# Splitting each output weight tile of part 2 into a low and a high half

## The chip, the cores and the metric

The kernel runs on one core of one Trainium2 chip. The metric is device time in microseconds (us) of one launch, as the median of several runs; the profile is one more execution, taken by the hardware profiler. A core has five engines that work beside each other, each with its own instruction queue: TensorE (PE in the profile, with its weight loads as PEld), VectorE (DVE), ScalarE (ACT), GpSimd (POOL) and SyncE (SP), which here issues nearly all DMAs. The tensors lie in the chip's memory (DRAM); the engines work on SBUF, and matmuls write to PSUM.

## The reference

`reference()` chains three stages, all float32:

```
k_p, v_p = mean of k, v over 8 neighbours along seq         # batch 8, heads 8, seq 576, dim 64
attn     = softmax(q @ k_p.T / 8) @ v_p
x        = attn as 4608 tokens x 512
h        = max(x @ w1, x @ w2, x @ w3); y = h @ w_out       # 512 -> 768 -> 512
out      = relu(y @ w_in) ** 2 @ w_out2                     # 512 -> 2048 -> 512
```

Weights are handed in as 64-bit numbers, which the kernel converts itself.

## The kernel before, in words

Every matmul operand is split in two: a high half rounded to the format the matrix engine reads (`F32R`), and a low half that holds the rest. A product of two split operands is three matmuls: high x high, high x low, low x high. `PARTS` (line 41) holds these pairs (a, c), with a for the stationary operand and c for the moving one; 0 is high and 1 is low.

Part 1 (to about 755 us) does attention and the first feed-forward block. On the side, `prepare_in` and `prepare_out` read the weights of the second block, form the seven combinations that a Strassen-like scheme (7 products in place of 8, for 2 x 2 blocks) needs, split them and store them to DRAM (`wi2_dram`, `wo2_dram`). A `wo2_dram` entry is one combination m for one quarter of the hidden width: 128 partitions x [u][half][256], 4 KB per partition.

Part 2 loops over 9 token blocks j of 512 tokens, and in each over 4 groups gr of the hidden width. `moe2_in` makes the seven input products of a group (84 matmuls of 128 x 256, line 669) and the squared relu of their sums. `moe2_out` then makes the group's output products, in the order of `OUT`: four in groups 0 and 1, ten in groups 2 and 3, so 28 in a block. Each output product

- splits its operand into g (ScalarE writes the high half, line 133, VectorE the low half, line 134; a ring of four);
- takes its weight tile (512 KB, high and low half of both u) from a ring of five, `wo_p`;
- does 12 matmuls (line 799) into one of five accumulators accA to accF: four with g high and weights high, four with g high and weights low, four with g low and weights high.

`fetch_group` puts the loads of the next group's tiles on SyncE's queue (`fetch_out`, line 601). A load waits there until the product that used its buffer is done, since the ring has only five buffers. SyncE also reads the next block's y (`load_y`, line 616, small pieces that follow group 2) and stores the output (line 755). SyncE works in order: whatever stands behind a waiting DMA waits too.

The order of the instructions on each engine isn't the order of the Python code. A planner (`schedule_with_timeline_sim=True`) takes the code's order as priority, simulates the program with its own cost estimates, and gives each engine the next instruction that is ready in that simulation. So input-product matmuls of the next group stand between output products where the planner expected an operand late. On the chip the order is fixed, and an engine waits where an operand is later than planned.

Of the kernel before, what the change touches and what calls it, by code (L numbers as in the profile page):

```python
# [11 lines left out]
F32R = mybir.dt.float32r  # L12
# [8 lines left out]
P = 128  # L21
# [19 lines left out]
PARTS = ((0, 0), (0, 1), (1, 0))  # L41
# [41 lines left out]
def as_f32(ap):  # L83
    return ap.bitcast(F32)
# [8 lines left out]
def attention_moe_kernel(ctx: ExitStack, tc: tile.TileContext, q, k, v, vn, w1, w2, w3, wo1, wi2, wo2, out):  # L93
    nc = tc.nc
# [12 lines left out]
    for sign, base in ((1, POOL * MID), (-1, POOL - 1 - POOL * MID)):  # L107
        nc.gpsimd.affine_select(
            out=sums, in_=sums, compare_op=ALU.is_ge, fill=0.0, base=base,
# [4 lines left out]
    wo2_dram = {  # L114
        (m, g, h): dram.tile([P, 2, 2, 256], F32, name=f"wo2_dram{m}_{g}_{h}")
        for m in range(1, 8) for g in range(2) for h in range(2)
    }
# [14 lines left out]
    def split_to(hi, lo, src, engine):  # L132
        nc.scalar.activation(hi, src, AF.Copy)  # L133
        engine.tensor_tensor(out=lo, in0=src, in1=as_f32(hi), op=ALU.subtract)  # L134

    def split(hl, src, engine=nc.vector):

        split_to(hl[:, 0], hl[:, 1], src, engine)
# [9 lines left out]
    def convert(raw_pool, raw, after=None):  # L148

        low, high = raw[:, :, 0], raw[:, :, 1]
        a = raw_pool.tile([P, 512], I32, tag="row", name="wbits", bufs=3)
        if after is not None:
            nc.gpsimd.tensor_copy(as_f32(a[:1, :1]), after[:1, :1])
        nc.scalar.activation(as_f32(a), as_f32(high), AF.Abs, scale=REBIAS)  # L160
        nc.scalar.activation(low, low.bitcast(U32), AF.Copy, scale=LOW_SCALE, bias=LOW_BIAS)
        nc.vector.scalar_tensor_tensor(
            out=a, in0=a, scalar=3, in1=low, op0=ALU.logical_shift_left, op1=ALU.bitwise_or
        )
        nc.vector.scalar_tensor_tensor(
            out=a, in0=high, scalar=-0x80000000, in1=a, op0=ALU.bitwise_and, op1=ALU.bitwise_or
        )
        return as_f32(a)

    def in_place(raw):  # L170
        return raw.rearrange("p a b -> p (a b)").rearrange("p (c a) -> p c a", c=2).bitcast(F32R)
# [254 lines left out]
    def store_second(dst, w):  # L426
        nc.sync.dma_start(out=dst, in_=as_f32(w))

    def prepare_out(raw, rows, f):

        half = KF2 // 2
        g, u, h = f % half // 4, f // 2 % 2, f % 2

        def store(m, hi, lo):
            for i, w in enumerate((hi, lo)):
                store_second(wo2_dram[m, g, h][:, u, i], w)

        rows.append(convert(raw_p, raw[0], now[0]))
        own = in_place(raw[0])
        l, r = slice(0, 256), slice(256, 512)  # L440
        if f >= half:
            split(own, rows[0], nc.gpsimd)
            store(2, own[:, 0, l], own[:, 1, l])
            store(3, own[:, 0, r], own[:, 1, r])
            return
        b2, b1 = rows
        c = raw_p.tile([P, 512], F32, tag="row", name="wsum", bufs=3)

        def combine(out, in0, in1):
            nc.vector.tensor_tensor(out=out, in0=in0, in1=in1, op=ALU.subtract)  # L450

        combine(c[:, l], b1[:, r], b1[:, l])
        combine(c[:, r], b2[:, r], b1[:, r])
        combine(b1[:, r], b2[:, r], c[:, l])
        combine(b2[:, r], b2[:, l], b1[:, r])
        split(own, b1, nc.gpsimd)
        store(1, own[:, 0, l], own[:, 1, l])
        store(6, own[:, 0, r], own[:, 1, r])
        hi, lo = b1.bitcast(F32R), c.bitcast(F32R)
        split_to(hi, lo, c, nc.gpsimd)  # L460
        store(5, hi[:, l], lo[:, l])
        store(7, hi[:, r], lo[:, r])
        hi, lo = b2[:, l].bitcast(F32R), b2[:, r].bitcast(F32R)
        split_to(hi, lo, b2[:, r], nc.gpsimd)
        store(4, hi, lo)
# [124 lines left out]
    wi2_t, wo2_t, yr_t, y_t = {}, {}, {}, {}  # L590
# [6 lines left out]
            wi2_t[p].append(w)  # L597

    def fetch_out(gr, m, h):
        w = wo_p.tile([P, 2, 2, 256], F32R, tag="wo2", name="wo2s")  # L600
        nc.sync.dma_start(out=as_f32(w), in_=wo2_dram[m, gr % 2, h])
        wo2_t.setdefault((gr, m, h), []).append(w)

    def shared_place(i, shape, name):
        return y_p.tile(shape, F32, tag=f"r{i}", name=name)
# [51 lines left out]
    wo_p = ctx.enter_context(tc.tile_pool(name="wo_p", bufs=5, reuse_waits="tile"))  # L657
# [33 lines left out]
    def moe2_in(j, gr):  # L691

        def unit(h, half):
            if half and gr < NG // 2:
                return shared_place(4 * gr + h, [P, T2], "a21")
            return c_p.tile([P, T2], F32, tag=f"c{2 * half + h}", name=f"c{2 * half + h}")

        def bank():
            return mm_ps.tile([P, T2], F32, tag="ps", name="ps")

        c = {(h, half): unit(h, half) for h in range(2) for half in range(2)}

        def only(m):
            ps = bank()
            product(ps, j, gr, m, first=True)
            return ps

        squared_there = squared_by_scalar if gr == NG - 1 else squared
        nc.scalar.activation(c[0, 0], only(1), AF.Copy)
        add(c[0, 1], only(6), c[0, 0])  # L710
        add(c[1, 0], only(7), c[0, 1])
        y = only(5)
        add(c[1, 1], y, c[1, 0])
        squared_there(c[1, 1])
        add(c[0, 0], only(2), c[0, 0])
        squared_by_scalar(c[0, 0])
        add(c[1, 0], only(4), c[1, 0])
        squared_by_scalar(c[1, 0])
        product(y, j, gr, 3)
        add(c[0, 1], y, c[0, 1])  # L720
        squared_there(c[0, 1])
        return c
# [11 lines left out]
    def operand(gr, m, h, c):  # L734

        k = gr % (NG // 2)
        if m == 7:
            kept[k, h, "s3"] = shared_place(4 * k + 2 + h, [P, T2], "s3")
            kept[k, h, "a21"] = c[h, 1]
            minus(kept[k, h, "s3"], c[h, 0], c[h, 1])  # L740
            return kept[k, h, "s3"]
        if m == 5:
            add(kept[k, h, "a21"], c[h, 1], kept[k, h, "a21"])
            return kept[k, h, "a21"]
        if m == 6:
            minus(kept[k, h, "s3"], c[h, 1], kept[k, h, "s3"])
            return kept[k, h, "s3"]
        if m == 3:
            minus(c[h, 0], c[h, 0], kept[k, h, "s3"])
            return c[h, 0]  # L750
        return c[h, 1 if m == 4 else 0]
# [5 lines left out]
    def evacuate(j, b, n):  # L757

        acc = made[b][0]
        if b in "AB" and n == HALF:  # L760
            q = made["q" + b] = c_p.tile([P, T2], F32, tag="q" + b, name="q" + b)
            nc.scalar.activation(q, acc, AF.Copy)
        if n < FULL[b]:
            return
        q = made["qA"]
        if b == "A":
            o = c_p.tile([P, T2], F32, tag="c3", name="o")
            nc.scalar.activation(o, acc, AF.Copy)
            store_out(j, 0, 0, o)
        elif b == "D":  # L770
            add(q, acc, q)
        elif b == "B":
            o = c_p.tile([P, T2], F32, tag="c2", name="o")
            add(o, acc, q)
            store_out(j, 1, 0, o)
        elif b == "E":
            add(q, acc, q)
            add(made["qB"], made["qB"], q)
            store_out(j, 1, 1, made["qB"])
        else:  # L780
            add(q, acc, q)
            store_out(j, 0, 1, q)
        del made[b]

    def moe2_out(j, gr, m, h, c):

        g = g_p.tile([P, 2, T2], F32R, tag="g", name="g")
        split(g, operand(gr, m, h, c))
        b = BANKS[m]
        if b not in made:  # L790
            made[b] = [acc_ps.tile([P, T2], F32, tag=f"acc{b}", name=f"acc{b}"), 0]
        bank, n = made[b]
        made[b][1] = n + 1
        w = wo2_t[gr, m, h].pop(0)
        k = 0
        for a, c in PARTS:
            for u in range(2):
                for i in range(2):
                    nc.tensor.matmul(  # L799
                        bank[:, i * 256 : (i + 1) * 256], lhsT=g[:, a, u * HT + i * P : u * HT + (i + 1) * P],  # L800
                        rhs=w[:, u, c], start=(n == 0 and k == 0),
                        stop=(n + 1 in (HALF, FULL[b]) and k == 11),
                        skip_group_check=(n >= HALF),
                    )
                    k += 1
        evacuate(j, b, n + 1)

    def fetch_group(gr):
        for m, h in OUT[gr >= NG // 2]:
            fetch_out(gr, m, h)  # L810
# [5 lines left out]
    for j in range(NB2):  # L816
        for gr in range(NG):
            more = j + 1 < NB2
            c = moe2_in(j, gr)
# [55 lines left out]
```

## Time and profile before

| | us |
|---|---|
| median of 3 runs | 1467.53 (1467.47 to 1467.97) |
| the profiled execution | 1472.47 |
| span of its profile | 1470.7 |
| PE busy | 1433.6 (97%) |
| DVE busy | 982.5 (67%) |
| ACT busy | 765.2 (52%) |
| output weight loads | 252 of 512 KB, 5.1 from issue to landing (median) |

The span runs from the first to the last instruction; the execution's own time adds what lies around it. Matmuls are pipelined, so the duration of a single one (some 0.28 us) is more than its share of the time; the pace is read from long runs of them.

### The profile page before, as it was taken

Reading aid. Unit: us, or ns where it says so; the run is one execution under the profiler, and the core shown is the slowest. Engines: PE = TensorE matmul, PEld = TensorE weight load, DVE = VectorE, ACT = ScalarE, POOL = GpSimd, SP = SyncE. Lnnn points to the kernel's source line nnn. Section 1 sums busy time; section 2 is a strip of 40 time slices with the busy share of each in tenths; the row PEclk is TensorE's granted clock in tenths of the full one; section 3 lists DMA queues with packets and bytes.
Section 4 is the critical chain, followed back from the end, with each engine's and each line's share of the span. In section 5 each row is a group of like instructions: output and inputs, shape, how many; then the busy total and the mean of one; then the engine's idle time right before and its main releaser. Section 6 shows DMA issues by size and latency. Waiting matters only on the chain.

```text
span 1470.7 us, 27579 instructions
## 1 busy us (share of the span) xinstructions
PE 1433.6 (97%) x10410; PEld 1411.6 (96%) x10410; DVE 982.5 (67%) x1778; ACT 765.2 (52%) x1983; POOL 180.6 (12%) x228
## 2 busy tenths in 40 slices
PE   7989999999999999999999999999999999999998
PEld 4879999999999999999999999999999999999998
DVE  5896466675675846756336767677777767686775
ACT  7795366665666656664323445354535344454443
POOL 3451022312322312221000000000000000000000
PEclk9999999999999999999999999999999999999999
DMA  6653135433444433333459847565666666565746
GB/s 224 194 164 103 53 132 163 161 105 127 153 151 154 131 134 123 114 101 116 149 189 340 288 152 261 169 232 208 222 226 230 230 215 218 202 228 193 264 150 209
DMA packets 118307, 263.94 MB, mean 179 GB/s; under 512 B 12672, under 2 KB 62848, under 8 KB 118176
## 3 DMA queue, kind: packets, MB, share of 16 engines
q1 hardware_dynamic: 111264, 252.75, 51.3%
q10 hardware_dynamic: 6912, 9.44, 1.8%
q8 instruction: 82, 1.34, 0.4%
q14 instruction: 49, 0.40, 0.1%
HBM read 213.91 MB, written 48.23 MB: 178 GB/s over the span
## 4 chain that ended last, share of the span: by engine, by line
PE 88%; DMA 6%; ACT 3%; DVE 2%; issue 1%; POOL 0%; SPq 0%; DVEq 0%; ACTq 0%; POOLq 0%
PE ps L513 28%; PE ps L669 23%; PE ps L532 10%; PE accB L799 7%; PE accA L799 6%; PE accF L799 3%; DMA wo2s<-wo_dram 3%; PE accE L799 3%; PE accD L799 2%; PE sc L353 2%; PE tr L381 2%; PE av L410 1%; ACT ss L358 1%; PE av L409 1%; DMA wraw<-in_w_dram 1%
## 5 line engine op out<-in xcount | busy, mean ns | idle before, releaser
L513 PE MATMUL ps<-x,w 128*128 128x384 f32 x2592 | 493.9, 341 | 3.0 <-ACT w L133 1.3
L513 PEld LDWEIGHTS ps<-x,w 128*128 128x128 f32 x2592 | 450.6, 189 | 5.6 <-ACT w L133 2.8
L669 PE MATMUL ps<-y,wi2s 128*128 128x256 f32 x3024 | 369.1, 277 | 0.4 <-DVE a L679 0.2
L669 PEld LDWEIGHTS ps<-y,wi2s 128*128 128x128 f32 x3024 | 355.7, 188 | 1.3 <-DVE a L679 0.7
L532 PE MATMUL ps<-h,wo 128*128 128x384 f32 x864 | 161.4, 338 | 2.7 <-POOL wo L134 1.8
L532 PEld LDWEIGHTS ps<-h,wo 128*128 128x128 f32 x864 | 148.9, 188 | 3.4 <-POOL wo L134 2.1
L679 DVE TENSOR_TENSOR c<-ps,c 128x512 f32<-128x512 f32 x144 | 98.5, 689 | 68.1 <-PE ps L669 67.2
L688 ACT ACTIVATE c<-c 128x512 f32<-128x512 f32 x90 | 55.7, 628 | 166.3 <-DVE c L679 165.1
L521 DVE TENSOR_TENSOR hm<-ps,hm 128x384 f32<-128x384 f32 x144 | 79.5, 552 | 69.2 <-PE ps L513 66.9
L133 ACT ACTIVATE g<-c 128x512 fp32r<-128x512 f32 x144 | 90.3, 627 | 63.1 <-DVE c L685 23.3
L799 PE MATMUL accB<-wo2s,g 128*128 128x256 f32 x864 | 113.1, 279 | 8.2 <-DMA wo2s<-wo_dram 6.9
L799 PE MATMUL accA<-wo2s,g 128*128 128x256 f32 x864 | 116.3, 277 | 0.0
L799 PEld LDWEIGHTS accB<-wo2s,g 128*128 128x128 f32 x864 | 105.3, 189 | 9.5 <-ACT g L133 5.4
L134 DVE TENSOR_TENSOR g<-c,g 128x512 fp32r<-128x512 f32 x144 | 98.7, 688 | 18.6 <-ACT g L133 18.5
L799 PEld LDWEIGHTS accA<-wo2s,g 128*128 128x128 f32 x864 | 107.2, 188 | 0.0
L358 ACT ACTIVATE ss<-sc,st 128x72 f32<-128x72 f32 (+1 forms) x320 | 98.1, 320 | 16.8 <-DVE st L355 14.2
L364 POOL TENSOR_TENSOR ss<-ss,st 128x432 f32<-128x432 f32 (+1 forms) x64 | 56.3, 880 | 262.4 <-DVE st L363 174.6
L413 DVE TENSOR_TENSOR xf<-av,xf 64x192 f32<-64x192 f32 (+1 forms) x112 | 50.8, 453 | 46.5 <-ACT xf L412 44.4
L385 DVE TENSOR_TENSOR pt<-tr,pt 72x192 fp32r<-72x192 f32 (+1 forms) x112 | 49.3, 449 | 41.4 <-ACT pt L384 40.2
L412 ACT ACTIVATE xf<-av 64x192 f32<-64x192 f32 (+1 forms) x112 | 45.4, 406 | 54.3 <-PE av L410 39.2
L133 ACT ACTIVATE h<-hm 128x384 fp32r<-128x384 f32 x72 | 37.7, 524 | 66.4 <-DVE hm L521 65.9
L133 ACT ACTIVATE g<-s 128x512 fp32r<-128x512 f32 x72 | 44.7, 630 | 40.9 <-DVE s L682 25.0
(105 smaller groups left out, 1980.3 us busy)
## 6 DMA issues: line engine op xcount, KB each, us to landing
wo2s<-wo_dram SPq DMA_DIRECT2D x252, 512.0 KB, 5.1
wi2s<-wi_dram SPq DMA_DIRECT2D x24, 512.0 KB, 9.0
wraw<-in_wo_dram SPq DMA_DIRECT2D x22, 512.0 KB, 3.8
wraw<-in_w_dram SPq DMA_DIRECT2D x18, 512.0 KB, 3.5
y_dram<-ys ACTq DMA_DIRECT2D x48, 192.0 KB, 2.1
wraw<-in_wi_dram SPq DMA_DIRECT2D x16, 512.0 KB, 3.5
wi_dram<-wraw SPq DMA_DIRECT2D x16, 512.0 KB, 3.8
wo_dram<-wraw SPq DMA_DIRECT2D x64, 128.0 KB, 2.0
```

The lines of the kernel that those rows point to most:

```text
L133: nc.scalar.activation(hi, src, AF.Copy)
L134: engine.tensor_tensor(out=lo, in0=src, in1=as_f32(hi), op=ALU.subtract)
L358: nc.scalar.activation(ss[:, i, h], src[:, i, h], AF.Exp, bias=st[:, 0, i, h : h + 1], accum_out=st[:, 1, i, h : h + 1],)
L364: nc.gpsimd.tensor_tensor(out=ss, in0=ss, in1=st[:, 2].rearrange("p g (h o) -> p g h o", o=1).to_broadcast([m, g, 2, SP]), op=ALU.mult,)
L413: nc.vector.tensor_tensor(out=xf[r], in0=av[r], in1=xf[r], op=ALU.add)
L513: nc.tensor.matmul(ps, lhsT=w1_t[f, e][:, a, kk * P : (kk + 1) * P], rhs=x[kk][:, c], start=(n == 0), stop=(n == 3 * KD - 1),)
L521: nc.vector.tensor_tensor(out=hm, in0=ps, in1=hm, op=ALU.max)
L532: nc.tensor.matmul(ps, lhsT=wo1_t[kk][:, a, d * P : (d + 1) * P], rhs=hs[kk][:, c], start=(n == 0), stop=(n == 3 * KF1 - 1),)
L669: nc.tensor.matmul(bank[:, u * HT : (u + 1) * HT], lhsT=wi2_t[2 * gr + u][i][:, a, o + kk * P : o + (kk + 1) * P], rhs=y_t[j][m][:, c, kk] ...
L679: nc.vector.tensor_tensor(out=out, in0=in0, in1=in1, op=ALU.add)
L688: nc.scalar.activation(c, c, AF.Relu)
L799: nc.tensor.matmul(bank[:, i * 256 : (i + 1) * 256], lhsT=g[:, a, u * HT + i * P : u * HT + (i + 1) * P], rhs=w[:, u, c], start=(n == 0 an ...
```

## The change

Each weight tile becomes two tiles of 256 KB, the low and the high half of its split. They come from two rings (two tags) of five buffers each, which together take as much SBUF as the one ring before. The layout in DRAM changes with it, from [u][half] to [half][u], so that a half is 2 KB in a row per partition. `fetch_out` loads the low half first. The product takes its terms in another order: g high x weights low, g high x weights high, g low x weights high.

```diff
         def store(m, hi, lo):
             for i, w in enumerate((hi, lo)):
-                store_second(wo2_dram[m, g, h][:, u, i], w)
+                store_second(wo2_dram[m, g, h][:, i, u], w)
...
     def fetch_out(gr, m, h):
-        w = wo_p.tile([P, 2, 2, 256], F32R, tag="wo2", name="wo2s")
-        nc.sync.dma_start(out=as_f32(w), in_=wo2_dram[m, gr % 2, h])
-        wo2_t.setdefault((gr, m, h), []).append(w)
+        pair = [None, None]
+        for i in (1, 0):
+            pair[i] = wo_p.tile([P, 2, 256], F32R, tag=f"wo2{i}", name="wo2s")
+            nc.sync.dma_start(out=as_f32(pair[i]), in_=wo2_dram[m, gr % 2, h][:, i])
+        wo2_t.setdefault((gr, m, h), []).append(pair)
...
-        for a, c in PARTS:
+        for a, c in ((0, 1), (0, 0), (1, 0)):
             for u in range(2):
                 for i in range(2):
                     nc.tensor.matmul(
                         bank[:, i * 256 : (i + 1) * 256], lhsT=g[:, a, u * HT + i * P : u * HT + (i + 1) * P],
-                        rhs=w[:, u, c], start=(n == 0 and k == 0),
+                        rhs=w[c][:, u], start=(n == 0 and k == 0),
```

## Rows read from the trace of the kernel before

**Rows 1.** The page's head and its line of the matrix engine.
```profile
span 1470.7 us, 27579 instructions
...
PE 1433.6 (97%) x10410; PEld 1411.6 (96%) x10410; DVE 982.5 (67%) x1778; ACT 765.2 (52%) x1983; POOL 180.6 (12%) x228
```

**Rows 2.** Chain of waits, part 2: start us, us, engine, tile, line, count.
```profile
842.60 8.98 PE ps L669 x79
...
923.62 9.66 PE ps L669 x85
...
936.73 2.72 PE accB L799 x24
...
1000.65 9.66 PE ps L669 x85
```

**Rows 3.** Waits of the matrix engine, 755 to 1471 us: total, times, longest.
```profile
PE accB L799 <- DMA wo2s<-wo_dram: 6.9, 4, 2.8
PE accD L799 <- DMA wo2s<-wo_dram: 1.7, 1, 1.7
PE accF L799 <- DMA wo2s<-wo_dram: 0.9, 3, 0.5
```

**Rows 4.** Timeline of PE, last group of the second block: start, us, instructions, [idle before].
```profile
903.88 1.07 PE L799 MATMUL accB<-wo2s,g 128*128 128x256 f32 x8
...
907.06 0.62 PE L799 MATMUL accA<-wo2s,g 128*128 128x256 f32 x4
...
914.53 1.30 PE L799 MATMUL accB<-wo2s,g 128*128 128x256 f32 x8 [2.78 <-DMA wo2s<-wo_dram]
```

**Rows 5.** Timeline of SP there; chain of waits, two loads from issue to landing.
```profile
906.34 0.32 SPq L601 DMA_DIRECT2D wo2s<-wo_dram  x1
...
907.70 0.80 SPq L601 DMA_DIRECT2D wo2s<-wo_dram  x2
...
907.70 6.69 DMA wo2s<-wo_dram
...
1452.70 4.56 DMA wo2s<-wo_dram
```

**Rows 6.** Line 601, the loads: duration of an issue (ns), issue to landing (us).
```profile
L601 SPq DMA_DIRECT2D wo2s<-wo_dram x252: 319/320/1337, 758.6 to 1459.7; - x126
...
DMA to landing us min/median/max: 3.3/5.1/8.0
```

**Rows 7.** Stretches: us, busy of PE, PEld, DVE, ACT, POOL, PEclk, DMA share, GB/s.
```profile
814.00:818.00 4.00, 3.89 (x34) 3.72 (x33) 2.10 (x4) 0.69 (x2) 0.00 (x0) 1.00 1.03 396
915.00:919.00 4.00, 4.00 (x24) 4.00 (x23) 2.28 (x4) 1.50 (x3) 0.00 (x0) 0.57 0.77 267
1458.00:1462.00 4.00, 4.00 (x23) 4.00 (x23) 0.69 (x1) 0.63 (x1) 0.00 (x0) 0.57 0.72 261
...
907.00:914.00 7.00, 4.75 (x42) 4.55 (x41) 6.88 (x12) 4.04 (x8) 0.00 (x0) 1.00 0.92 265
```

**Rows 8.** Lines 799 and 669: separate wait instructions, count and ns.
```profile
L799 PEldq EVENT_SEMAPHORE  x237: 51/51/51, 767.0 to 1463.0; - x119
...
L669 PEldq EVENT_SEMAPHORE  x48: 51/51/51, 752.5 to 1441.4; - x48
```

**Rows 9.** Third group of block 923.62: SP's issues, SP's wait, PE's tenth product.
```profile
966.14 0.32 SPq L601 DMA_DIRECT2D wo2s<-wo_dram  x1
...
SPq L616 <- DMA wo2s<-wo_dram: 1.4, 1, 1.4
...
975.44 1.09 PE L669 MATMUL ps<-y,wi2s 128*128 128x256 f32 x8
976.37 1.53 PE L799 MATMUL accF<-wo2s,g 128*128 128x256 f32 x12
```

**Rows 10.** DMA of 770 to 784 us and of 962 to 973 us.
```profile
DMA packets 1781, 5.65 MB, mean 404 GB/s; under 512 B 200, under 2 KB 200, under 8 KB 1778
...
DMA packets 1756, 2.94 MB, mean 267 GB/s; under 512 B 189, under 2 KB 1195, under 8 KB 1756
```

## The prediction

> **What bounds the kernel now.** I read four views in this order. The page first: the matrix engine is busy for 1433.6 of 1470.7 us [rows 1], so nothing on another engine or in a queue pays unless it ends an idle stretch of that engine, or brings its clock back. Then the chain of waits, for the length of a token block of part 2. A block begins where a run of 85 input-product matmuls starts: 842.60 and 923.62 are two blocks apart by 81.02 us, 923.62 and 1000.65 by 77.03 us [rows 2]. The 77.03 us block has no wait of the matrix engine in it; 672 matmuls at the pace of its long run (9.66 us / 85 = 113.6 ns) are 76.4 us. So a clean block is at the engine's pace, and a block that is longer has lost the rest. The whole loss of part 2 to output weights is in the third view, the waits of the matrix engine: 6.9 us in accB (4 times), 1.7 in accD (once), 0.9 in accF (3 times), together 9.5 us in 8 waits [rows 3].
>
> The fourth view is the timeline around the longest of them. In the last group of a block (ten products) the seventh product, accB, sat 2.78 us until its weight tile landed [rows 4]. The ring has five tiles, so that tile takes the buffer of the group's second product: accA, whose last 4 matmuls start at 907.06 and are over near 907.7. SyncE issued the load at 907.70, and it landed 6.69 us later; in the last block the same load took 4.56 us [rows 5]. The loop is: a buffer is held for the whole product, the load of 512 KB takes a median 5.1 us (3.3 to 8.0) [rows 6], and five products further on take 5 x 1.36 = 6.8 us (2.72 us for two [rows 2]). Loop and cover are nearly equal, and the jitter of the landing decides. That is why only some blocks wait.
>
> A wait has a second price. The granted clock was 1.00 right after the 1.72 us wait of accD, but 0.57 on average in 915 to 919 us, after the 2.78 us wait, and 0.57 in 1458 to 1462 us, after the last block's wait of 2.00 us [rows 7]; 0.57 is a mix of the 1.2 and the 2.4 GHz level. Each of the two stretches loses 4 x 0.43 = 1.7 us, 3.4 us in all. Block 842.60 to 923.62 agrees: 81.02 - 77.03 = 4.0, against 2.78 + 1.7 = 4.5. So what the output weights cost is 9.5 + 3.4 = 12.9 us, 0.9% of the time. No more can be won from them.
>
> **The change, part by part.**
>
> *Layout in memory and stores.* The stores of part 1 write the same 1 KB per partition to another place in the same 4 KB row. Count, size and order stay; I take 0.
>
> *Order of the terms.* The first eight matmuls of a product still use g's high half and the last four its low half, so the waits for ScalarE and VectorE stay where they are. New is that the low half of the weights is read by the first four matmuls only. Its buffer comes free after a third of the product: in the first product of the group (8 matmuls from 903.88 with others between, and its buffer refilled at 906.34 [rows 4, 5]) near 903.88 + 4 x 0.11 + 0.1 = 904.4 in place of 906.3, 1.9 us sooner; in a product whose 12 matmuls follow each other, 0.9 us sooner. The high half's buffer is free when the whole tile was. And the high half is needed four matmuls, 0.45 us, after the product starts.
>
> *What that does to the waits.* Take the 2.78 us one. The high half of tile 7 goes out at 907.70 as before, but of the 1 MB that was on its way in tiles 6 and 7, the low half of tile 6 (256 KB) has left the queue, and the low half of tile 7 was issued up to 0.9 us before and has partly left. 256 to 512 KB at the 265 GB/s of 907 to 914 us [rows 7] are 1.0 to 2.0 us; I take 1.5. With 0.45 us of later need the wait shrinks by about 1.95 us: 2.78 to 0.8, and the other waits of the last group (0.88, 1.23 and 2.00 us in accB, two of 0.17 us in accF) to nothing. The two in the first block stand in a stretch where the queues run full, 396 GB/s [rows 7]; there an earlier issue is worth less, and I give 0.45 us and half of 0.9 us: 1.72 to 0.8, 0.51 to 0. Left over: 1.6 us of 9.5, so 7.9 us are gained. A wait of 0.8 us is below the 1.72 us that left the clock at 1.00, so both clock losses go: 3.4 us more. Bounds of this part: 0, if the landings move with the issues, to 12.9 us.
>
> *252 more DMA issues.* One costs SyncE 0.32 us [rows 6], 252 x 0.32 = 81 us over some 710 us of part 2. SyncE isn't behind: it issued at 907.70 what came free near 907.7 [rows 4, 5], so its waits for buffers hide this; if they didn't, in a burst of two tiles the last half would go out 2 x 0.45 us later (the pair at 907.70 took 0.80 us for two [rows 5]), which the DMA engines can't use sooner anyway, since 512 KB at 404 GB/s [rows 10] are 1.3 us. I take 0.
>
> *252 more waits on the matrix engine*, one before the fifth matmul of each product. Behind it stand the other eight matmuls, and all that the engine has in order after them. Satisfied, such a wait is carried by the matmul or by a separate instruction of 51 ns: bounds 0 to 252 x 0.051 = 12.9 us. The nearest rows say 0: the output products have 237 of these instructions for 252 products, the input products 48 for 252 [rows 8], and both run at the same pace (2.72 us / 24 = 113.3 ns against 113.6 [rows 2]). I take 0.
>
> *Sum.* The profiled execution took 1472.47 us for its span of 1470.7: 1472.47 - 7.9 - 3.4 = 1461.2 us. The runs' median, 1467.53, is 4.94 us under it. If the profiled execution had 4.94 us of the waits that the timed runs don't have, the runs come to 1461.2 too; if they have all of them, to 1467.53 - 11.3 = 1456.2. The spread of the runs, 0.5 us, shows that what they have repeats, not how much; I lean to the first end: **1460 us**. What is late next is nothing in a clean block; elsewhere it is ScalarE, whose waits at line 799 are under 1 us.
>
> **The rivals.**
>
> *A. The waits move.* The order on each engine is written by a planner from its own estimates of when loads land. In the group before the last, 8 input matmuls stand ahead of the tenth product [rows 9], and 5 ahead of the ninth, although g was ready; I read that as the planner expecting the weights late. With loads that it sees earlier it may take those 13 x 0.11 = 1.5 us out, and the wait of the last group turns up in this one: some 1 us in each of 8 blocks, 8 of the 11.3 us given back. 1464.6 to 1470.4, about 1467. For it: only five tiles fit either way, and bytes per block don't change. Against it: the landing itself gets 1 to 2 us of slack.
>
> *B. Slower: eight DMAs in flight.* In the third group the 128 and 64 KB reads of y stand among the weights. The read issued at 971.64 us had waited 1.4 us for a weight load [rows 9], and the load issued eight DMAs before it is the one of 966.14. So there seems to be a limit of eight, and a half counts as a whole. Between 962.9 and 969.7 us 15 DMAs went out; with halves 20 want to, against 8 in flight at the 3.3 us of the quickest loads [rows 6], 2.4 per us: 8.3 us, so the last half goes out near 971.2 in place of 969.2 and lands 3.3 to 5.1 us later, by 976.3. The tenth product starts at 976.37 [rows 9] and needs it 0.45 us later, so this decides when that landing takes over 5.6 us, or when A takes the cover away as well. Then 1.7 us in each of 8 blocks, 13.6 us, less the gain of 6.3 in the runs: +7, 1475 us. For it: the limit shows, 8.0 us landings exist. Against: the early low halves start before the y reads, and five prefetched tiles cover half of the group.
>
> *C. Smaller transfers are slower.* The first stretch with 512 KB loads moved 404 GB/s, the one with y reads 267 GB/s [rows 10]. If halves went at the second rate, the five late tiles of a group of ten, 2.6 MB, would take 9.8 us in place of 6.5: 3.3 us more in some nine groups, less the gain: up to +20 us, about 1485. Against: these rows differ in what SyncE waits for as well as in size. The Trainium skill (DMA: Bandwidth & Descriptors, Rules for kernel authors) speaks against the change here: it asks for 1 MiB or more per DMA for full bandwidth. By that rule the time would be C's; the trace doesn't bear it out, since loads of half that size already ran at 404 GB/s [rows 10].
>
> *D. It doesn't do what it says:* the planner queues each low half behind the high half before it, which waits for the whole product. The first low half of a group still goes early, so half of the gain stays: 1464.
>
> **Chances.** Forecast 0.52 (own range 1455 to 1463.5), A 0.22, B 0.14, C 0.04, D 0.08. A measurement here can tell 0.2%, 2.9 us. The forecast and most of D are faster, a tenth of A too: 0.60. Same: the rest of A, a little of D and B: 0.22. Slower: B and C: 0.18. Range: 12.9 us below the median is 1454.6; above, A whole and the lower part of B: 1455 to 1471.
>
> **What would show it.** Right: no wait over 1 us for weights in the last groups, no stretch below full clock after 840 us, blocks of 77.0 us throughout, low halves issued 1 to 2 us before their high halves, 504 issues of 256 KB. Wrong: waits for weights in the third groups (A, B), reads of y held for a weight load longer than 1.4 us (B), landings of halves as long as 5.1 us (the first bound), the pace of output products over 113.6 ns (the added waits).

## The result and the profile after

The change made the kernel slower: a median of 1481.35 us (1476.52 to 1484.67, 5 runs) against 1467.53 (1466.91 to 1470.17), ratio 1.0085 [1.0066, 1.0104]. In a second comparison it was 1483.51 against 1472.14 us, 1.0082 [1.0059, 1.0106]. The forecast was 1460 us in a range of 1455 to 1471. The profiled execution took 1481.35 us.

What follows compares stretches, since the length of part 1 differs from execution to execution. Part 2 starts with a run of 30 input matmuls: at 755.77 us in the profile before, at 758.21 after. The 2.4 us between them arise in the first 165 us, from loads that land at other times; the matrix engine has the same order there, and the stores in the new layout begin only at 220 us. In the 14 profiles of this case, which share part 1's order, part 2 starts between 755.6 and 759.1 us. Counted from that start to the end of the span, part 2 took 714.9 us before and 720.8 after (723.7 in the second profile of the change). That is 6 to 9 us of the 11 to 14 us between the medians; where the rest lies isn't shown.

The page and the chain of waits after the change, to set beside [rows 1, 2]:

```profile
span 1479.0 us, 28106 instructions
...
PE 1432.1 (97%) x10410; PEld 1410.1 (95%) x10410; DVE 985.0 (67%) x1778; ACT 765.9 (52%) x1983; POOL 181.4 (12%) x228
```
```profile
758.21 3.42 PE ps L671 x30
...
923.16 9.66 PE ps L671 x85
...
936.27 2.72 PE accB L801 x24
...
1002.31 9.66 PE ps L671 x85
...
1080.06 9.66 PE ps L671 x85
...
1159.72 9.66 PE ps L671 x85
```

The lines have moved by two, so the products are line 801 and the loads line 603. The pace is what it was (9.66 us for 85 matmuls, 2.72 for 24). But blocks now take 79.15, 77.75 and 79.66 us, where a clean one took 77.03. Where the time went is in the waits of the matrix engine (total, times, longest), to set beside [rows 3]:

```profile
PE accB L801 <- DMA wo2s<-wo_dram: 15.7, 9, 2.6
PE accB L801 <- ACT qB L764: 0.7, 1, 0.7
PE ps L671 <- ACT c L711: 0.3, 1, 0.3
```

Before, 9.5 us of waits for weights stood in accB, accD and accF. Now there are nine waits, all in accB, one in the last group of each block (0.66 to 2.59 us), 15.7 us. Each stands at the product's fifth matmul, the first that reads the high half. The waits of accD and accF are gone. The 6.2 us more of waits are about what part 2 grew by. Here is the same group as in [rows 4], on the matrix engine, after the change:

```profile
906.09 1.07 PE L801 MATMUL accE<-wo2s,g 128*128 128x256 f32 x8
907.00 0.62 PE L801 MATMUL accA<-wo2s,g 128*128 128x256 f32 x4
907.45 0.62 PE L801 MATMUL accE<-wo2s,g 128*128 128x256 f32 x4
907.90 1.07 PE L801 MATMUL accA<-wo2s,g 128*128 128x256 f32 x8
908.81 1.07 PE L801 MATMUL accD<-wo2s,g 128*128 128x256 f32 x8
909.72 0.62 PE L801 MATMUL accA<-wo2s,g 128*128 128x256 f32 x4
910.17 0.62 PE L801 MATMUL accB<-wo2s,g 128*128 128x256 f32 x4
913.07 0.74 PE L801 MATMUL accB<-wo2s,g 128*128 128x256 f32 x4 [2.28 <-DMA wo2s<-wo_dram]
913.64 3.16 PE L801 MATMUL accD<-wo2s,g 128*128 128x256 f32 x16
916.60 1.05 PE L801 MATMUL accB<-wo2s,g 128*128 128x256 f32 x4
```

And the kernel before, from the same place in the group:

```profile
908.87 1.07 PE L799 MATMUL accD<-wo2s,g 128*128 128x256 f32 x8
909.78 0.62 PE L799 MATMUL accA<-wo2s,g 128*128 128x256 f32 x4
910.23 1.52 PE L799 MATMUL accD<-wo2s,g 128*128 128x256 f32 x12
```

Before, after accA x4 came accD x12 (the last four of the fifth product and the first eight of the sixth), and then the seventh product, accB. After the change the planner puts accB ahead: its four matmuls with the low half at 910.17, whose weights have landed, and right behind them the four with the high half, whose weights have not. Sixteen matmuls of accD stand behind that wait now, and none passes it; before, twelve of them ran from 910.23 without a wait. The high half of the seventh tile is wanted 1.0 us before the whole tile was: the wait begins at 913.07 - 2.28 = 910.79, before at 914.53 - 2.78 = 911.75 [rows 4].

After the change all nine last groups stand in this order. The kernel before had it once, in its last block, and the 2.00 us wait of that block is at this place:

```profile
1457.39 1.45 PE L799 MATMUL accB<-wo2s,g 128*128 128x256 f32 x8 [2.00 <-DMA wo2s<-wo_dram]
1458.64 3.35 PE L799 MATMUL accD<-wo2s,g 128*128 128x256 f32 x16
```

The load of the high half gained nothing, on average, to pay for this. SyncE's queue issued it at 907.64, as before, when the second product released its buffer; the low half of the seventh tile went out at 905.38. From issue to landing (chain of waits of the change):

```profile
907.64 5.38 DMA wo2s<-wo_dram
...
988.40 5.24 DMA wo2s<-wo_dram
...
1067.64 3.77 DMA wo2s<-wo_dram
...
1145.58 5.48 DMA wo2s<-wo_dram
...
1303.10 5.69 DMA wo2s<-wo_dram
...
1461.82 4.79 DMA wo2s<-wo_dram
```

With 4.22 at 1225.12 and 5.28 at 1384.16, the eight in blocks 2 to 9 average 5.0 us for 256 KB. Before, the whole tile of 512 KB took 6.69, 4.79, 5.27 and 4.56 us at this place in the four blocks that waited for it, 5.3 on average. But those are the late ones. The landing of every load can be worked out from the semaphore events in the trace (16 for each load; "worked out" below means this). Over all nine blocks the whole tile took 4.5 us on average and the half takes 4.8.

One difference between the two is what is still on its way when the load goes out. Before, that was 512 KB in every block, the sixth tile. Now it is 768 KB in seven of the nine: the seventh tile's low half, the sixth's high half, and the eighth's low half, which went out at 906.74, ahead of the half that is needed first. The view over the loads, to set beside [rows 6]:

```profile
L603 SPq DMA_DIRECT2D wo2s<-wo_dram x504: 319/326/1710, 760.9 to 1467.9; - x168
...
DMA to landing us min/median/max: 2.9/4.6/8.6
```

Its last line, like that of [rows 6], rests on the loads whose landing the view could tell, 66 of 504 here and 28 of 252 there. Worked out for all, 256 KB took a median 4.6 us (2.5 to 8.6), and 512 KB 5.3 us (3.1 to 10.8).

The clock fell again behind some of the waits, to set beside [rows 7] (columns as there):

```profile
913.00:917.00 4.00, 3.93 (x22) 3.93 (x23) 1.02 (x3) 1.25 (x3) 0.00 (x0) 0.65 0.91 314
1308.00:1314.00 6.00, 5.16 (x31) 5.16 (x32) 3.02 (x6) 2.30 (x4) 0.00 (x0) 0.72 0.90 301
993.00:998.00 5.00, 4.32 (x36) 4.32 (x37) 3.26 (x6) 2.31 (x4) 0.00 (x0) 1.00 0.95 320
```

After 2.28 us of waiting at 913 it was 0.65 on average, after 2.59 us at 1308 0.72, both mixes of the 1.2 and the 2.4 GHz level; after 2.14 us at 993 it stayed at 1.00. The two slow stretches lose 4 x 0.35 = 1.4 and 6 x 0.28 = 1.7 us, about as much as the two before [rows 7], and no other stretch of part 2 is slow while matmuls run; so what the change adds is the waits themselves.

### The profile page after: what moved, and what is told of

The parts are those of the page before. It is cut to its first block, busy times and chain, and to the rows that moved or that the text cites. A ratio compares the mean times of both kernels' runs of the same rounds, so it can differ in the third digit from the quotient of the medians.

```text
span 1479.0 us, 28106 instructions
## 1 busy us (share of the span) xinstructions
PE 1432.1 (97%) x10410; PEld 1410.1 (95%) x10410; DVE 985.0 (67%) x1778; ACT 765.9 (52%) x1983; POOL 181.4 (12%) x228
## 4 chain that ended last, share of the span: by engine, by line
PE 89%; DMA 5%; DVE 2%; ACT 2%; issue 1%; POOL 0%; SPq 0%; DVEq 0%; POOLq 0%; ACTq 0%
PE ps L513 28%; PE ps L671 23%; PE ps L532 10%; PE accB L801 7%; PE accA L801 6%; PE accF L801 3%; PE accE L801 3%; PE accD L801 3%; DMA wo2s<-wo_dram 3%; PE sc L353 2%; PE tr L381 2%; PE av L410 1%; PE av L409 1%; ACT ss L358 1%; DMA kr<-in_k_dram 1%
## 5 line engine op out<-in xcount | busy, mean ns | idle before, releaser
L801 PE MATMUL accB<-wo2s,g 128*128 128x256 f32 x864 | 115.9, 279 | 16.4 <-DMA wo2s<-wo_dram 15.7
L358 ACT ACTIVATION_READ_ACCUMULATOR ss<-sc,st 128x1 f32 (+1 forms) x320 | 65.8, 206 | 0.0
```

Source lines behind the costliest of these rows:

```text
L358: nc.scalar.activation(ss[:, i, h], src[:, i, h], AF.Exp, bias=st[:, 0, i, h : h + 1], accum_out=st[:, 1, i, h : h + 1],)
L801: nc.tensor.matmul(bank[:, i * 256 : (i + 1) * 256], lhsT=g[:, a, u * HT + i * P : u * HT + (i + 1) * P], rhs=w[c][:, u], start=(n == 0 an ...
```

## The experiments

Twelve runs were made, in three sessions; each session compares with runs of the kernel before on its own chip, whose medians were 1472.1 to 1472.4 us. Lengths of part 2 are counted from its start, as above.

**Theory 1 (order):** the loss comes from the seventh product standing ahead of the sixth on the matrix engine. **Theory 2 (transfers):** 504 loads of 256 KB land late, whatever the order.

**e1: the change with its order mended.** `issue_after` fixes only an order on one engine; it adds no wait. `mark` is the product's eighth matmul.

```diff
-        for a, c in ((0, 1), (0, 0), (1, 0)):
+        with tc.issue_after(eighth[0]) if eighth else ExitStack():
+            for a, c in ((0, 1), (0, 0), (1, 0)):
...
+                        if k == 8:
+                            mark = ins
+        eighth[:] = [getattr(mark, 'ins', mark)]
```

> The change, with the matrix engine's order mended: the first matmul of each output product is queued behind the eighth of the product before, so the seventh product of a block's last group (accB) can't go ahead of the sixth (accD). Theory 1 (order): the planner hoisted the seventh product because its low half lands early in the planner's estimate, and the chip then waits for the high half, which goes out no sooner than before. The 15.7 us of waits for weights (9 waits in accB) fall below 6 us, the clock stays at full speed in the last groups, and the time is 1460 to 1470 us, at least 8 us under the change's 1481. Theory 2 (transfers): loads of 256 KB land late whatever the order. Waits stay above 12 us, time 1476 to 1485 us.

Measured: 1469.33 us, 0.9977 [0.9964, 0.9989] of before; part 2 711.7 us. The planner's order in the last group went back to accD x12, accB x8 and was new only from the eighth product on. The waits of e1:

```profile
PE accB L804 <- DMA wo2s<-wo_dram: 3.5, 7, 1.0
PE accE L804 <- DMA wo2s<-wo_dram: 3.2, 7, 0.8
```

They fell from 15.7 to 6.7 us (6 were expected at most, a near miss), none over 1.02 us, and the clock stayed at full speed to the end of part 2. With the halves kept and only the order changed, about 1% came back (9 to 12 us of it in part 2). This is theory 1. But the gain on the kernel before is 3 us, not the 11 of the prediction.

**e3: two loads a tile, one ring.** The kernel before with the change's layout and order of terms, each tile filled by two loads, pinned as e1.

```diff
-        nc.sync.dma_start(out=as_f32(w), in_=wo2_dram[m, gr % 2, h])
+        for i in (1, 0):
+            nc.sync.dma_start(out=as_f32(w[:, i]), in_=wo2_dram[m, gr % 2, h][:, i])
...
-                        rhs=w[:, u, c], start=(n == 0 and k == 0),
+                        rhs=w[:, c, u], start=(n == 0 and k == 0),
```

> Only the split of the load: one ring of five tiles of 512 KB as before, each filled by two loads of 256 KB (low half first), the change's order of terms and layout in DRAM, and the same pin of the products' order. No half is released early. Theory 1: near the kernel before, 1465 to 1472 us, waits for weights 5 to 12 us. Theory 2 (504 loads of 256 KB cost by themselves): 1476 us or more, waits above 14 us.

Measured: 1471.87 us, 0.9994 [0.9982, 1.0007]; waits for weights 4.8 us. In this order 504 loads show no cost by themselves, in SyncE's queue or on the way. Theory 2 falls. (Single loads of 512 KB with the same pin weren't run.)

**e4: the early place alone.** The kernel before, whole tiles, pinned as e1, but with the sixth and the seventh product exchanged in the last group. (The sums of accD and accB then meet in another sequence, so a part of the output lacks a summand; the amount of work is the same.)

```diff
+            turn = list(OUT[gr >= NG // 2])
+            if gr == NG - 1:
+                turn[5], turn[6] = turn[6], turn[5]
```

> The kernel before, whole tiles of 512 KB, but with the seventh product of the last group put ahead of the sixth on the matrix engine (the loads keep their order). The seventh tile is needed some 0.9 us sooner and lands as before. Theory 1: the waits for weights grow from 9.5 us by about 0.9 us in each of 9 blocks to 14 to 20 us, with clock losses behind the longer ones: 1474 to 1482 us, the slowdown of the change without its halves. Theory 2: the order doesn't matter, 1465 to 1470 us.

Measured: 1480.14 us, 1.0047 [1.0033, 1.0061]; part 2 722.0 us. The waits of e4 on the matrix engine:

```profile
PE accB L802 <- DMA wo2s<-wo_dram: 10.3, 7, 2.7
PE accB L802 <- ACT y L133: 4.2, 2, 2.2
PE accB L802 <- ACT g L133: 2.1, 2, 1.4
```

A wait goes to whichever operand came last by the profile. Those put down to ScalarE (y, g) end 0.14 us after a weight load landed (worked out), just as those put down to loads do, so all three lines are waits for weights, 16.6 us. The seventh product waited 1.3 to 2.7 us in each of blocks 2 to 9, and the slowdown came without any half. By the medians this is about half of the change's 0.8%; part 2 of this profile is as long as the change's (720.8 and 723.7 us). The change has its seventh product further ahead still (16 matmuls of accD behind the wait, 12 here); whether that makes the difference isn't shown.

**e2: the order of the terms alone.**

```diff
-        for a, c in PARTS:
+        for a, c in ((0, 1), (0, 0), (1, 0)):
```

> Only the order of the terms: the kernel before with g high x weights low first. Tiles, rings, loads and layout as before, so the planner's order of the engines should not move. Both theories: 1466 to 1471 us, no change. Were it slower by over 5 us, the order of terms would cost by itself and both theories lack it.

Measured: 1472.35 us, 0.9996 [0.9983, 1.0010]; part 2 714.8 us, as before. The planner's order didn't move.

**r1: the change again,** beside e5, e6 and e9.

> The change as it is, beside the next kernels on one chip, so that they can be compared. 0.6 to 1.1% over the kernel before, one wait for weights in accB in the last group of nearly every block, 12 to 20 us together.

Measured: 1483.51 us, 1.0082 [1.0059, 1.0106]; ten waits in accB, 18.0 us.

**e5: four low, six high buffers, order not mended.** Asks whether the wait is counted from the release of the high half's buffer.

```diff
-            pair[i] = wo_p.tile([P, 2, 256], F32R, tag=f"wo2{i}", name="wo2s")
+            pair[i] = wo_p.tile([P, 2, 256], F32R, tag=f"wo2{i}", name="wo2s", bufs=4 if i else 6)
```

> The change with the same SBUF dealt out anew: four buffers for low halves, six for high halves. The planner still puts the seventh product of the last group ahead of the sixth (its order there is the change's), but its high half takes the buffer of the group's first product, which comes free one product (1.36 us) sooner. Theory 1 (the wait is the high half's landing, counted from the release of its buffer, against an early place in the order): the nine waits shrink by about 1.36 us each, 15.7 us to 3 to 7 us, time 0.992 to 1.001 of before. Rival (the transfers are limited by the rate of the DMA engines in that stretch): an earlier issue doesn't help, waits stay above 11 us, ratio 1.005 or more.

Measured: 1470.09 us, 0.9990 [0.9973, 1.0008], against the change's 1.0082 in the same session; part 2 709.2 us. The same group in e5:

```profile
908.43 1.07 PE L801 MATMUL accD<-wo2s,g 128*128 128x256 f32 x8
909.34 0.62 PE L801 MATMUL accA<-wo2s,g 128*128 128x256 f32 x4
910.04 1.18 PE L801 MATMUL accB<-wo2s,g 128*128 128x256 f32 x8
911.06 2.05 PE L801 MATMUL accD<-wo2s,g 128*128 128x256 f32 x16
```

The seventh product still stands ahead of accD, and it hardly waits: its high half went out at 905.90, when the first product was done, with 512 KB still on their way ahead of it in place of 768, and took 3.3 us (worked out). The waits for weights of the whole run are 3.7 us, and those left stand at the first matmul of a product, which reads the low half. An earlier issue does help, so the rival falls as it was stated. The time of issue and what lies ahead changed together here, so the run doesn't show that the rate has no part.

**e6: e5 with the order of e1.**

> As the run before, with the products' order pinned as well (the seventh behind the eighth matmul of the sixth). Theory 1: the waits of the pinned kernel, 6.7 us with a longest of 1.0, go nearly away (under 3 us), ratio 0.992 to 0.996. Rival (rate of the transfers): waits as in the pinned kernel, ratio 0.997 to 0.999.

Measured: 1470.55 us, 0.9987 [0.9974, 1.0000]; waits for weights 5.4 us, most of them (3.8 us) now in accF, the eighth and tenth products. A miss: with two remedies the waits didn't go, and the ratio is in the rival's range. The waits moved on to the products behind. All of them stand at the first matmul of a product, which reads the low half, where in e1 nearly all stood at the fifth: with four buffers the low halves are the late ones.

**e9: three low, seven high buffers, order of e1.**

> Three buffers for low halves, seven for high halves, order pinned. The planner now expects low halves late and puts 7 to 13 input matmuls between output products, which is cover. Theory 1: the waits go nearly away too unless a low half, released later, takes their place: 0.991 to 0.997. Rival (rate): 0.997 to 1.000. Were the low halves the new wait, the waits would stand at the first matmul of products and the ratio be over 1.000.

Measured: 1490.21 us, 1.0127 [1.0105, 1.0149]; waits for weights 17.6 us, in all five accumulators. The cover that the planner added didn't help. All 21 waits stand at the first matmul of a product: with three buffers the low halves come late, the sign that the expectation named for a ratio over 1.000.

**e10: fewer low halves.** The change without the low loads of the last three tiles of each last group; those products read the high half in place of the low one, so part of the output is another.

> The change, but the low halves of the last three tiles of each last group aren't loaded; their products read the high half in their place (part of the output is not the reference's). The order of the matrix engine around the seventh product is the change's. It asks why the high half of the seventh tile lands no sooner than a whole tile did (about 5.0 us from its issue in the change's profile, 5.3 for the whole tiles of before). If the low halves that now go out early share the DMA engines with it, it lands in 3.3 to 4.2 us and the nine waits in accB fall below 9 us. If the landing of a load has little to do with what else is on its way, it stays near 5 us and the waits stay at 13 to 20 us.

Measured: 1485.24 us in one run; waits in accB 16.8 us in 11. The load of the seventh high half took 5.18, 4.88, 5.73, 4.64, 5.15, 5.38 and 3.63 us in seven of the nine blocks. By the expectation the landing doesn't depend on the low halves. But SyncE's queue shows ten loads from 905.74 to 912.09 us in this group too: the free low buffers were filled with the next group's tiles. The stretch had as many loads under way as in the change, so this run does not tell the two apart.

The traces of the two kernels go further. In part 2 a load that went out with nothing else on its way took 3.4 us on average for 512 KB (25 loads) and 2.6 us for 256 KB (28 loads); with exactly 1 MB ahead of it, 5.2 us (51 loads) and 4.7 us (75 loads), all worked out. So a half does land sooner by itself, by 0.8 us, but what is ahead of it counts for more. This compares places in the kernel that differ in other ways too; no run changed only what is ahead.

**e7: products whole.** As e1, but each product's first matmul stands behind the twelfth of the product before.

```diff
-                        if k == 8:
+                        if k == 12:
```

> The change with a stronger pin: the first matmul of each output product is queued behind the twelfth of the product before, so products stand whole on the matrix engine and buffers come free in the order of need (the first two tiles of a group some 1.0 us sooner). Theory 1 (order): no product ahead of its turn, waits for weights below 4 us, 0.990 to 0.997 of before. Rival: g's low half, which the interleaving hid, becomes the wait before the ninth matmul, over 0.3 us in most products: ratio over 1.000.

Measured: 1460.54 us (1459.62 to 1462.25), 0.9914 [0.9894, 0.9935] of before, faster than both kernels; part 2 703.4 us. Its waits and the last group of the second block, beside the rows above:

```profile
PE ps L671 <- DVE c L681: 1.2, 2, 0.9
PE accB L804 <- ACT qB L764: 0.7, 1, 0.7
PE accE L804 <- DMA wo2s<-wo_dram: 0.4, 1, 0.4
...
PE accF L804 <- DMA wo2s<-wo_dram: 0.2, 1, 0.2
```
```profile
902.56 1.52 PE L804 MATMUL accB<-wo2s,g 128*128 128x256 f32 x12
903.92 1.76 PE L804 MATMUL accA<-wo2s,g 128*128 128x256 f32 x12
905.51 1.52 PE L804 MATMUL accE<-wo2s,g 128*128 128x256 f32 x12
906.87 1.52 PE L804 MATMUL accA<-wo2s,g 128*128 128x256 f32 x12
908.23 2.88 PE L804 MATMUL accD<-wo2s,g 128*128 128x256 f32 x24
910.95 1.52 PE L804 MATMUL accB<-wo2s,g 128*128 128x256 f32 x12
```

Products stand whole and in order. The second product ends 3.1 us after the group's start, not 3.8, and the seventh starts 8.4 us after it, not 6.4 as in the change (910.17 - 903.82). Of waits for weights 0.6 us are left. The rival of the expectation, waits for g's low half, did not come: the longest the weight loads of line 804 show is 0.3 us.

**e8: e7 with four low and six high buffers.**

> The run before with four buffers for low and six for high halves. Theory 1: waits under 2 us, 0.989 to 0.996. Rival as in the run before.

Measured: 1466.98 us, 0.9956 [0.9942, 0.9971]; waits for weights 5.1 us, a miss, all at the first matmul of a product. Worse than e7: with products in order, five and five is the better deal.

**e11: whole products, whole tiles.** The kernel before with the pin of e7.

> The kernel before (whole tiles of 512 KB, one ring) with the same strong pin, to see what the pin does without halves. Theory 1: buffers come free sooner here too, so the waits of 9.5 us fall to 3 to 8 us, 0.993 to 0.999; the halves then are worth the difference to the run with halves, some 0.2%. Rival (g's low half): over 1.000.

Measured: 1470.41 us, 0.9978 [0.9961, 0.9994]; waits for weights 4.2 us, part 2 711.8 us. So the strong pin alone is worth 0.2%. The halves are worth 0.2% with e1's pin (e1 against e3, 1469.33 and 1471.87 us), and 0.7%, 9.9 us, with the strong pin (e7 against e11; the planner spread the input matmuls a little differently in the two). Some 0.2% was expected, a miss; the pin and the halves together give 0.86%, more than the two gains added up. Why isn't shown.

## Why the prediction was wrong

*What bounds the kernel.* Right. Waits for output weights were what part 2 lost, and no more than that could be won: in e7, which has almost none, part 2 takes 703.4 us, 11.5 us less than in the kernel before, where the prediction counted 11.3 of at most 12.9.

*Order of the terms: the step that failed.* "The first eight matmuls of a product still use g's high half [...] so the waits for ScalarE and VectorE stay where they are." They did. What did not stay is the place of the products. I worked out when the halves would land against an order of the matrix engine that I took from the kernel before, although that order is written by a planner that sees the loads; the price of a new order was nothing in this term, without a reason. A low half that lands sooner let it put the seventh product ahead of the sixth, and 16 matmuls that use other tiles then stood behind the wait for the high half. e1 against r1 prices this at about 1%, some 15 us, and turns the slowdown into a gain of 0.2%; e4 shows the early place slowing the kernel before, where there are no halves. The trace of the kernel before had a sign of it: its last block already stood in this order, and the prediction took its 2.00 us wait for the same case as the others. That the planner did it because its estimate has the high half landing in time is an inference from the order that it wrote; its estimates weren't looked at.

*The wait shrinks by 1.95 us.* Mis-sized as well. The 1.5 us of sooner landing were 256 to 512 KB less on the way in tiles 6 and 7. The sum left out the eighth tile's low half, which now goes out ahead: 768 KB were on their way when the high half was issued, where it had been 512 KB. Over the nine blocks it took 4.8 us where the whole tile had taken 4.5; in the block that the prediction worked through, 5.38 in place of 6.69. Landings of halves as long as 5.1 us were one of its signs of being wrong. So even in the order of e1 3.5 us of waits stay in accB, and another 3.2 in accE, the ninth product, which the planner also put ahead. That what is on its way ahead makes up for the smaller size fits all loads of the two traces, but e10, which was to test it, doesn't. What helps in this place is to issue the load sooner (e5, e7).

*The two waits in the first block.* 1.72 and 0.51 us were to shrink to 0.8 and nothing. Both went, but one of 0.66 us came in accB, from the new order.

*252 more issues and 252 more waits.* Right at 0. The pace is the same, line 801 has 236 separate waiting instructions, and e3 with all of the loads and most of the waits runs like the kernel before.

*The rivals.* A was the nearest: the planner did move its order. Its first half is in the trace: in the group before the last, the 15 to 18 input matmuls that stood between the late products in blocks 2 to 8 are down to one or none. But no wait came there, against the place and the price that I gave; the loss was in the last group, and a product that goes ahead is not a cover that is taken away. (Its 1464.6 to 1470.4 us are the band of 0.2% around the median; 8 us on 1456.2 to 1461.2 give 1464.2 to 1469.2.) Of B, SyncE's loads and reads did wait for loads under way (9.0 us in 23 and 8.2 us in 20 times; before 11.8 us in 13 and 12.5 us in 14), but after the change the matrix engine never waited in a third group of the blocks 2 to 9. (14 DMAs went out in its stretch, not 15.) C falls with e3, which took the time of the kernel before with 504 loads of 256 KB. The 267 GB/s that it was worked out from is a mean over a stretch whose first 1.6 us moved nothing. The rule that spoke for C (the Trainium skill, DMA: Bandwidth & Descriptors, Rules for kernel authors: 1 MiB or more per DMA for full bandwidth) shows no effect here, at 0.9994 [0.9982, 1.0007]. D didn't happen: low halves of tiles 6 and 7 went out at 904.47 and 905.38, ahead of the high half at 906.28.

*How the numbers follow.* I read the 0.5 us between three runs as a kernel that repeats itself. Later sets of 21 to 29 runs of the same kernel spread by 8 to 11 us; the profiles show part 1's first 165 us and the waits for weights differing from one execution to the next. And what I had forecast as likeliest came from waits that existed; a new order could make new ones, and I gave too little chance to that.

## What to carry to other kernels

Where a planner writes the order of an engine, a change that makes one operand ready sooner can change the order too, and the engine, whose order is fixed on the chip, then waits for the rest of that operand (here with 16 matmuls of other tiles behind each wait). Ask of each split operand what will now be put ahead and which part of it is still to come; if the gain was worked out in a fixed order, fix that order with the change (here worth 0.2 to 0.9% with the halves). A ring is paid from release to landing, and landing went here with what was on its way ahead as well as with size: count that too. Finishing the products in their order and halving the loads were worth 0.2% each, and 0.9% together.

## What the runs showed of the hardware

- A load of 256 KB took a median of 4.6 us from issue to landing in part 2 (the change), one of 512 KB 5.3 us (before), worked out for all loads. With nothing else on its way it was 2.6 and 3.4 us on average, with 1 MB ahead 4.7 and 5.2 us.
- The granted clock fell towards the 1.2 GHz level (0.91 on average over 20 us) after a wait of 2.04 us (r1, at 1229 us) and one of 1.96 us (e4, at 1071 us), and stayed at 2.4 GHz after 2.14 and 2.38 us (the change, at 994 and 1151 us): the length of the wait alone doesn't decide.
- Fourteen profiles with one order of the matrix engine in part 1 are up to 3.4 us apart at 165 us, where loads and the first products meet, and stay as far apart to the end of part 1.
